# A linear-attention block and a gated MLP on one core: an x load cut in two, and the written-out instruction order searched again

## Chip, core and metric

The kernel runs on one core of one Trainium2 chip. The metric is device microseconds of one execution. The core has five engines that each work through their own instruction queue: TensorE (PE, matmuls, with its weight loads shown as PEld), VectorE (DVE), ScalarE (ACT), GpSimd (POOL) and SyncE (SP, which here only issues DMAs). They meet at semaphores alone.

## The reference

x is 2048 x 512 in bfloat16. Cut to what matters:

```python
x = A_x
h = x + A(layernorm(x))
out = h + B(layernorm(h))

def A(x):                       # 32 heads of 16
    q, k, v = split(x @ wqkv)
    pq, pk = phi(q), phi(k)     # phi(t) = where(t > 0, t + 1, exp(t)) + 1e-6
    kv, z = pk^T v, sum_s pk
    return ((pq kv) / (pq z + 1e-6)) @ wo

def B(x):                       # 1792 = 2 * 896
    z = gelu(x @ w_in)
    z1, z2 = z[:, :896], layernorm(z[:, 896:])
    return (z1 * (w_sp @ z2 + b_sp)) @ w_out
```

## The kernel before

The 2048 rows are 16 tiles of 128. Everything stays in SBUF. The stages, with the short names that the text uses and the line of the instruction:

- **Loads.** SP issues x tile 0, x tile 1, x tiles 2 and 3, the K weights `wk`, x 4 and 5, x 6 and 7, x 8 to 11, x 12 to 15, and the Q weights `wq`, in that order (`load_x`, `load`, L492). The other weights are loaded by POOL after the last x transpose has landed.
- **First layer norm.** For each tile, DVE takes `stats` (L567) and `aggr` (L571). The reciprocal root comes from ACT for tiles 0 to 3 (L581, L583) and from POOL for pairs of tiles from 4 on (`rstd_pool`: an add, L586, and a power, L588). DVE then makes `norm` (L603). Tiles 0 to 5 are transposed by PE (`T0` to `T5`, L633) and copied by ACT (`cp0` to `cp5`, L640). Tiles 6 to 15 are transposed by DMAs from SP (`T6` to `T15`, L625).
- **Attention.** `k0` to `k15` are the K projections of the tiles (L715, four matmuls each). They come in pairs, and `phi` of a pair goes through ACT (L692, L694) and DVE (L695, then L698 or L701). `kx` (L747, two matmuls each) accumulates k^T x of a tile and a half. `q0.0` to `q3.3` are the Q projections of a group of four tiles (L729), with their own `phi`. Then come the denominator (`den`, L829 and L844, with DVE L856 and L859 after it), the product with the values (L796), the output matrix (L814) and `o0` to `o15` (L879), whose residual is added on DVE (`resid`, L884).
- **Second layer norm.** `stats`, `aggr`, `rstd_pool`, and `minus` on POOL (L614, L615) give a bias, with which ACT makes `norm_h` (L610). SP transposes by DMA (`Th0` to `Th15`, L625).
- **MLP.** `z2` of a tile (L911) goes through GELU on ACT (L916), `stats` on DVE (L920), a reciprocal root on POOL and `norm` on DVE. `z1` (L942) is made by columns, with GELU at L947. `mix` (L981, 16 matmuls per 128 columns) multiplies with w_sp, DVE gates (L988), and `out` (L999) makes the result, to which DVE adds h (L1005).

PSUM has eight banks. A matmul group that needs a bank waits until the last reader of the bank's previous tile is done. POOL's reciprocal roots, ACT's copies and all else run in queue order: an instruction that waits holds up all behind it.

What each engine does next is written out, as a search made beforehand left it: `ORDER` is one list of all 803 operations, and each engine's queue is that list filtered by engine. `SLOT` gives each tile its place (a PSUM bank, an SBUF buffer). `schedule()` walks `ORDER` with the costs given to `op(...)` and a clock, but the clock only fills `start` and `end`. Queues, slots and waits follow from `ORDER`, `SLOT` and the data alone.

```python
for o in (self.ops[i] for i in ORDER):
    ...
    o.start, o.end = t, t + o.cost + o.lag
    ...
    order[o.eng].append(o)
```

Of the kernel before, what the change touches and what calls it, by code (L numbers as in the profile page):

```python
# [7 lines left out]
ACT = mybir.ActivationFunctionType  # L8
ALU = mybir.AluOpType
# [3 lines left out]


ORDER = [
# [36 lines left out]
]  # L52
SLOT = [
# [6 lines left out]
]  # L60


# [292 lines left out]
def bass_sequential_preLN__linear_attn_block__mixer_gmlp__prompt_kernel(  # L355
# [63 lines left out]
    pk = View(s_kv, 0, [NT, D], BF16)  # L419
# [18 lines left out]
    zb = small([KD * CG], BF16)  # L438
    sel = small([P], BF16)
    ones = small([CG], BF16)  # L440
    part = small([CG], BF16)
# [18 lines left out]
    zr_v = View(s_wsp, NT * GW * 2, [D], BF16)  # L460
# [18 lines left out]
    op = g.op  # L479
# [4 lines left out]
    def act_c(n, ptr=0):  # L484
        return 0.055 + 0.000833 * n + 0.093 * ptr
# [16 lines left out]
    def load_x(eng, a, b, bias=BIG, **kw):  # L502
        more = {2: 103e3, 4: 70e3}.get(a, 0)
        xl[a] = load(eng, f"x{a}", x[a:b, :], x_dram[a * P:b * P, :].rearrange("(n p) d -> p n d", p=P),
                     int((b - a) * P * D * 2 + more), bias, **kw)
# [4 lines left out]
    load("sp", "wk", wqkv[:, D:2 * D], w3[:, :, D:2 * D], D * D * 2 + 50000)  # L510
    for a in (4, 6):
        load_x("sp", a, a + 2)
    for a in (8, 12):
        load_x("sp", a, a + 4)
    load("sp", "wq", wqkv[:, 0:D], w3[:, :, 0:D], D * D * 2)
    for a, b in zip(g.ops, g.ops[1:]):
        b.after.append(a)
# [4 lines left out]
       r=[ident.all()], w=[ident.all()], bias=BIG)  # L522
# [62 lines left out]
    def rstd_pool(var, dst, n):  # L585
        op("pool", 0.25, lambda e: e.tensor_scalar(dst.ap(), var.ap(), EPS_LN, None, op0=ALU.add), r=[var], w=[dst])  # L586
        h = nhalf[0:n]
        return op("pool", 0.35, lambda e: e.tensor_tensor(dst.ap(), dst.ap(), h.ap(), ALU.pow), r=[dst, h], w=[dst],  # L588
                  lag=0.45)

    def stats_act(n):
        src, s1, nm, s2 = x[n, :], st_x[n, 0:1], st_x[n, 6:7], st_x[n, 7:8]
# [14 lines left out]


    def normalise_act(dst, src, rs, nm, n=512):
        op("act", act_c(n, 2), lambda e: e.activation(dst.ap(), src.ap(), ACT.Identity, bias=nm.ap(), scale=rs.ap()),  # L610
           r=[src, rs, nm], w=[dst])

    def minus(m, rs, nm):
# [33 lines left out]
    for grp in LN1:  # L647
        rs = small([len(grp)], FP32)
# [88 lines left out]
    for p in range(NP):  # L737
        t = kv_proj(p, D)
# [15 lines left out]
    tz = Tile(PS)  # L754

    def zsum(e):
# [2 lines left out]
            i = e.matmul(tz(bank(0)).ap()[CG * c:CG * (c + 1), :], lhsT=ones.ap, rhs=pk.ap[:, n, :],  # L759
                         start=(n < KD), stop=(n >= NT - KD), skip_group_check=True)  # L760
        return i
    op("pe", 1.02, zsum, r=[pk.all(), ones.all()], w=[tz()])
    for f in (0, 2):
        q_proj(0, f)

# [1 line left out]
       w=[zr_v.all()])  # L767
    tzT = Tile(PS)

    def zmm(e):  # L770
# [1 line left out]
            i = e.matmul(tzT(bank(0)).ap()[:, c * CG:(c + 1) * CG], lhsT=zr_v.ap[:, c * P:(c + 1) * P], rhs=part.ap,  # L772
                         start=(c == 0), stop=True, skip_group_check=True)
        return i
    op("pe", 0.25, zmm, r=[zr_v.all(), part.all()], w=[tzT()])

    def zmask(e):
        z = tzT(bank(0)).ap()[:, 0:KD * CG].rearrange("p (c f) -> p c f", c=KD)
# [4 lines left out]
    for h in range(2):  # L783
        d = xk_v[2 * h:2 * h + 2, :]
        if h == 0:
            op("act", act_c(1024), lambda e, h=h, d=d: e.activation(d.ap(), txk[h]().ap(), ACT.Copy), r=[txk[h]()],
               w=[d])
# [21 lines left out]
    for b in range(2):  # L809
        t = Tile(PS, 2)  # L810
        for i in range(2):
            c = 2 * b + i
            r_ = wo[c, :]
            op("pe", MM, lambda e, t=t, i=i, c=c, r_=r_: e.matmul(  # L814
                t(bank(i)).ap(), lhsT=kvT.ap()[:, c * P:(c + 1) * P], rhs=r_.ap(), start=True, stop=True),
               r=[kvT, r_], w=[t()])
# [6 lines left out]
    def den(gq):  # L823
        t = Tile(PS)
        r_ = pqT[gq].all()

        def mm(e):
            for c in range(KD):
                i = e.matmul(t(bank(0)).ap()[CG * c:CG * (c + 1), :], lhsT=zb.ap[:, CG * c:CG * (c + 1)],  # L829
                             rhs=r_.ap()[:, c, :], start=True, stop=True)  # L830
            return i
        op("pe", 0.33, mm, r=[zb.all(), r_], w=[t()])
        rr, rb = rr_v[gq, :], rb_v[gq, :]
        op("act", act_c(512, 1), lambda e: e.activation(rr.ap(), t(bank(0)).ap(), ACT.Ln, bias=eps[1:2].ap(),
                                                        scale=1.0), r=[t(), eps[1:2]], w=[rr])
        o = op("act", act_c(512), lambda e: e.activation(rb.ap(), rr.ap(), ACT.Exp, scale=-1.0), r=[rr],
               w=[rb])
        last_lnexp.append(o)
        spread = {0: Tile(PS, 2), 2: Tile(PS, 2)}

        def sp_(e):
# [2 lines left out]
                k = e.matmul(spread[c // 2 * 2](bank(c % 2)).ap(), lhsT=sel.ap[q0:q0 + CG, :],  # L844
                             rhs=rb.ap()[q0:q0 + CG, :], start=True, stop=True)
            return k
        op("pe", 0.33, sp_, r=[sel.all(), rb], w=[spread[0](), spread[2]()])
        for c0 in (0, 2):
            t2 = spread[c0]
            d = pqT[gq][c0:c0 + 2, :]  # L850
            if (gq, c0) in VIA_ACT:
# [3 lines left out]
                   r=[t2()], w=[b_])  # L855
# [13 lines left out]
    for gq in range(NG):  # L869
        g.bias = -GROUP * gq  # L870
        for p in (2 * gq, 2 * gq + 1):
            t = Tile(PS, 2)
# [205 lines left out]
```

## Time and profile before

| what | value |
|---|---|
| median of 3 runs | 245.82 us (244.99 to 247.24) |
| the profiled execution | 246.68 us |
| its span, first to last instruction | 244.9 us |
| granted TensorE clock | 1.00 |
| DVE, ACT, POOL busy | 135.5, 85.0, 32.8 us |
| matmuls, start to start in a full run of them | 0.216 us for 512 columns, 0.162 for 384 |

The profile is of one execution. Its page gives busy time by engine, its chain of waits follows the work back from the last instruction, the wait view says which engine stood idle for whom, and the timeline gives each instruction's start, duration, idle time before it in brackets and what ended that idle time. Windows give busy time per engine in a stretch. The view of DMA issues gives the time from issue to landing.

### The profile page before, as it was taken

The page shows a single profiled execution, that of the slowest core. Times are in us where ns is not written, and L with a number is a line of the kernel's source. Part 1 is how long each engine was busy: PE and PEld are TensorE (multiplying, and loading weights), DVE is VectorE, ACT ScalarE, POOL GpSimd, SP SyncE. Part 2 cuts the span into 40 slices and gives each one's busy share as a digit, 9 for nine tenths or more (in the row PEclk, how much of TensorE's full clock was granted, in tenths as well). Part 3 has the DMA queues.
Part 4 walks back from the last instruction along what each step waited for, and adds up shares of the span by engine and source line. Part 5 has one row for each costly group of instructions (what it writes and reads, how often), then busy time and mean ns, then how long its engine had stood idle before and what let it go on. Part 6 is the DMA issues. An engine that isn't in the chain of part 4 may idle for free.

```text
span 244.9 us, 3021 instructions
## 1 busy us (share of the span) xinstructions
PE 238.6 (97%) x1175; PEld 108.5 (44%) x1175; DVE 135.5 (55%) x269; ACT 85.0 (35%) x107; POOL 32.8 (13%) x87
## 2 busy tenths in 40 slices
PE   8798999999999998999999999999999999999995
PEld 3343443353444444444444444444444444444443
DVE  4899655679999694688523132252332523322443
ACT  3674756787599936855501100000000000000000
POOL 5114130000525305133200000000000000000000
DMA  6903368943123530479544454445000110000022
GB/s 199 313 4 74 80 122 332 252 106 67 35 55 64 120 72 3 88 210 146 90 95 103 94 84 104 107 98 137 3 0 0 46 43 0 0 0 3 0 86 86
DMA packets 55582, 21.57 MB, mean 88 GB/s; under 512 B 49456, under 2 KB 54704, under 8 KB 55568
## 3 DMA queue, kind: packets, MB, share of 16 engines
q1 hardware_dynamic: 54624, 17.05, 31.9%
q0 software_dynamic: 944, 4.33, 5.3%
q8 instruction: 9, 0.15, 0.3%
q14 instruction: 5, 0.04, 0.0%
HBM read 7.47 MB, written 2.10 MB: 39 GB/s over the span
## 4 chain that ended last, share of the span: by engine, by line
PE 73%; DVE 13%; ACT 5%; DMA 4%; POOL 2%; issue 1%; SPq 1%
PE ps L981 39%; PE ps L999 10%; PE ps L942 5%; PE ps L911 5%; DVE small L567 4%; PE ps L729 4%; PE ps L747 4%; DVE xh L884 3%; DMA xh<-in_A_x_dram 3%; PE ps L715 3%; ACT xn L610 2%; PE ps L879 2%; DMA xT_pq_z<-pk_xn_z 1%; DVE small L920 1%; POOL small L588 1%
## 5 line engine op out<-in xcount | busy, mean ns | idle before, releaser
L981 PE MATMUL ps<-wsp,pk_xn_z 128*128 128x512 bf16 x336 | 73.5, 379 | 0.0
L988 DVE TENSOR_TENSOR e<-ps,e 128x512 bf16<-128x512 f32 x28 | 19.4, 692 | 68.7 <-PE ps L981 68.7
L981 PEld LDWEIGHTS ps<-wsp,pk_xn_z 128*128 128x128 bf16 x336 | 32.9, 98 | 39.6
L942 PE MATMUL ps<-hT,win 128*128 128x512 bf16 x112 | 26.5, 379 | 0.7 <-ACT pk_xn_z L916 0.7
L911 PE MATMUL ps<-win,hT 128*128 128x512 bf16 (+1 forms) x128 | 26.2, 353 | 0.0
L999 PE MATMUL ps<-wout,xT_pq_z 128*128 128x512 bf16 (+1 forms) x119 | 24.7, 366 | 0.0
L981 PE MATMUL ps<-wqkv_wsp,pk_xn_z 128*128 128x512 bf16 x112 | 24.3, 379 | 0.0
L567 DVE BATCH_NORM_STATS2 small<-xh 128x6 f32<-128x512 bf16 x32 | 21.0, 681 | 4.0 <-DMA xh<-in_A_x_dram 3.8
L920 DVE BATCH_NORM_STATS2 small<-pk_xn_z 128x6 f32<-128x512 bf16 (+1 forms) x32 | 18.4, 611 | 7.7 <-ACT pk_xn_z L916 7.6
L692 ACT ACTIVATE e<-ps 128x1024 bf16<-128x1024 f32 x16 | 16.4, 1026 | 12.3 <-PE ps L715 6.5
L947 ACT ACTIVATE xT_pq_z<-ps 128x1024 bf16<-128x1024 f32 (+1 forms) x16 | 14.2, 911 | 18.5 <-PE ps L942 18.5
L911 PEld LDWEIGHTS ps<-win,hT 128*128 128x128 bf16 x128 | 12.5, 98 | 12.6 <-issue 0.2
L1005 DVE TENSOR_TENSOR e<-ps,xh 128x512 bf16<-128x512 f32 (+1 forms) x17 | 11.2, 660 | 11.3 <-PE ps L999 11.2
L999 PEld LDWEIGHTS ps<-wout,xT_pq_z 128*128 128x128 bf16 x119 | 11.7, 98 | 12.7
L916 ACT ACTIVATE pk_xn_z<-ps 128x896 bf16<-128x896 f32 x16 | 14.5, 916 | 7.7 <-PE ps L911 7.6
L981 PEld LDWEIGHTS ps<-wqkv_wsp,pk_xn_z 128*128 128x128 bf16 x112 | 11.0, 98 | 13.2
L942 PEld LDWEIGHTS ps<-hT,win 128*128 128x128 bf16 x112 | 10.7, 98 | 13.7 <-ACT pk_xn_z L916 1.7
L715 PE MATMUL ps<-wqkv_wsp,xT_pq_z 128*128 128x512 bf16 x64 | 15.8, 379 | 0.7 <-DMA xT_pq_z<-pk_xn_z 0.7
L588 POOL TENSOR_TENSOR small<-small 128x2 f32<-128x2 f32 x22 | 16.0, 732 | 1.3
L747 PE MATMUL ps<-pk_xn_z 128*128 128x512 bf16 x64 | 15.9, 379 | 0.0
L729 PE MATMUL ps<-xT_pq_z,wqkv_wsp 128*128 128x512 bf16 x64 | 15.6, 379 | 0.1
L879 PE MATMUL ps<-pk_xn_z,xT_pq_z 128*128 128x512 bf16 x64 | 14.8, 379 | 0.0
(72 smaller groups left out, 180.8 us busy)
## 6 DMA issues: line engine op xcount, KB each, us to landing
out_dram<-e SPq DMA_DIRECT2D x15, 128.0 KB, 1.7
win<-in_B_w_in_dram POOLq DMA_DIRECT2D x1, 1792.0 KB, 8.3
wqkv_wsp<-in_A_wqkv_dram SPq DMA_DIRECT2D x2, 512.0 KB, 6.3
xh<-in_A_x_dram SPq DMA_DIRECT2D x2, 512.0 KB, 7.1
wout<-in_B_w_out_dram POOLq DMA_DIRECT2D x1, 896.0 KB, 6.4
xh<-in_A_x_dram SPq DMA_DIRECT2D x3, 256.0 KB, 4.4
wsp<-in_B_w_sp_dram SPq DMA_TRANSPOSE x48, 3.0
wqkv_wsp<-in_A_wqkv_dram POOLq DMA_DIRECT2D x1, 512.0 KB, 8.8
```

What stands on the lines that cost most here:

```text
L567: op("dve", dve_c(512), lambda e: e.bn_stats(s6.ap(), src.ap()), r=[src], w=[s6])
L588: return op("pool", 0.35, lambda e: e.tensor_tensor(dst.ap(), dst.ap(), h.ap(), ALU.pow), r=[dst, h], w=[dst], lag=0.45)
L715: i = e.matmul(t(bank(ti)).ap(), lhsT=lhs.ap()[:, c, :], rhs=rhs.ap()[:, c, :], start=(c == 0), stop=(c == KD - 1))
L729: r_ = e.matmul(t(bank(i)).ap(), lhsT=lhs.ap()[:, c, :], rhs=rhs.ap()[:, c, :], start=(c == 0), stop=(c == KD - 1))
L747: r = e.matmul(txk[h](bank(i)).ap(), lhsT=xx.ap()[:, c * P:(c + 1) * P], rhs=kk.ap(), start=(n == 0), stop=(n == NT - 1))
L879: i = e.matmul(t(bank(ti)).ap(), lhsT=l.ap()[:, c, :], rhs=mw[c, :].ap(), start=(c == 0), stop=(c == KD - 1))
L911: k = e.matmul(t(bank(i)).ap()[:, 0:b - a], lhsT=l.ap()[:, c, :], rhs=win[c, a:b].ap(), start=(c == 0), stop=(c == KD - 1))
L920: op("dve", dve_c(b - a), lambda e, s6=s6, src=src: e.bn_stats(s6.ap(), src.ap()), r=[src], w=[s6])
L942: k = e.matmul(t(bank(i)).ap(), lhsT=l.ap()[:, c, :], rhs=r_.ap()[:, c, :], start=(c == 0), stop=(c == KD - 1))
L981: k = e.matmul(t(bank(0)).ap(), lhsT=l.ap()[:, s - a, :], rhs=r_.ap()[:, s - a, :], start=(s == 0), stop=(s == NT - 1))
L988: op("dve", dve_c(512), lambda e: e.tensor_tensor(gb().ap(), t(bank(0)).ap(), bsp().ap()[:, tg * GW:(tg + 1) * GW], ALU.add), r=[t(), bsp( ...
L999: k = e.matmul(t(bank(0)).ap()[:, 0:b - a], lhsT=l.ap()[:, fc, :], rhs=wout[fc, a:b].ap(), start=(fc == 0), stop=(fc == KF - 1))
```

## The change

One load becomes two. The rest of the SP queue is the same.

```diff
-    for a in (8, 12):
-        load_x("sp", a, a + 4)
+    for a in (8, 10):
+        load_x("sp", a, a + 2)
+    load_x("sp", 12, 16)
```

Costs that `schedule()`'s clock reads are edited: POOL's power from 0.35 with a lag of 0.45 to 0.7, `normalise_act` by +0.04, the small matmul groups L759, L772, L829 and L844 to 0.88, 0.1, 0.23 and 0.23 with other landing times.

```diff
-        return op("pool", 0.35, lambda e: e.tensor_tensor(dst.ap(), dst.ap(), h.ap(), ALU.pow), r=[dst, h], w=[dst],
-                  lag=0.45)
+        return op("pool", 0.7, lambda e: e.tensor_tensor(dst.ap(), dst.ap(), h.ap(), ALU.pow), r=[dst, h], w=[dst])
```

`ORDER` and `SLOT` are replaced as wholes. Because of the added load, operations from number 7 on are one higher. The same 803 other operations are there, each on its engine. Decoded into the names above, the queues differ most in these stretches (an arrow marks where a queue goes on):

```
PE  before: T0 warm warm T1 warm k0 warm T2 k1 T3 k2 T4 k3 T5 k4 kx0.1 kx1.1 q0.2 q0.3 k5 q0.0 kx2.1 kx3.1 q0.1
            kx0.0 kx1.0 kx2.0 kx3.0 kx4.0 k6 k7 kx4.1 kx5.1 kx5.0 q1.2 q1.3 k8 k9 ->
PE  after:  T0 warm warm T1 warm warm k0 T2 k1 k2 T3 T4 T5 k3 k4 q0.0 q0.1 k5 kx0.0 kx0.1 kx1.1 kx1.0 q0.2 q0.3
            kx2.0 kx3.0 kx2.1 kx3.1 k6 k7 kx4.1 kx5.1 q1.2 q1.3 kx4.0 kx5.0 q1.0 q1.1 kx6.0 k8 k9 ->
DVE before: stats6 stats11 norm4 norm5 phi_k0 aggr6 phi_k0 stats10 stats8 aggr11 stats7 stats13 aggr7 phi_k1
            stats14 phi_k1 norm6 aggr14 norm7 ->
DVE after:  stats6 stats7 norm4 norm5 aggr6 aggr7 phi_k0 stats15 phi_k0 norm7 stats12 aggr15 norm6 phi_k1 stats11
            aggr12 stats9 stats8 stats13 aggr8 aggr13 phi_k1 phi_k2 stats10 phi_k2 ->
POOL before (2nd layer norm, pairs): h0 h1, h3 and h2 mixed, h5, h4 and z0 mixed, bsp load, z2, h7 and h6 mixed, z4 ->
POOL after: h0 h1 h2, bsp load, h3 h6, add h4, minus h4, power h4, add z0, add z2, add h7, power z0, power h7,
            minus h7, minus h4, minus h7, power z2, h5, z4 ->
ACT after:  ... norm_h8 norm_h9 gelu1_1.6 gelu1_1.4 gelu2_7 norm_h14 gelu2_4 norm_h10 ->
PE  after, late: ... z2_6 z2_5 z1_1.6 z1_1.4 z1_1.5 z2_7 z2_4 z1_1.2 z1_1.3, first four matmuls of mix 0.0 ->
```

In the later part, the Q projections run in the order q0, q1, q3, q2 (before: q0 to q3), and the first `mix` group, which is cut into pairs of matmuls, starts among the `z2` of tiles 6 to 9 (before: after nearly all of `z2`). From `mix` 0.1 on both orders are the same but for four `z1` groups that stood behind `mix` 0.3, of which one remains, behind `mix` 0.5. POOL's constants at the start are in another order; the identity for the PE transposes is next to last but one.

More of the change, by code (lines that the diff above doesn't have):

```diff
@@ L609, in normalise_act @@
     def normalise_act(dst, src, rs, nm, n=512):
-        op("act", act_c(n, 2), lambda e: e.activation(dst.ap(), src.ap(), ACT.Identity, bias=nm.ap(), scale=rs.ap()),
+        op("act", act_c(n, 2) + 0.04, lambda e: e.activation(dst.ap(), src.ap(), ACT.Identity, bias=nm.ap(), scale=rs.ap()),
            r=[src, rs, nm], w=[dst])
@@ L761, in zsum @@
         return i
-    op("pe", 1.02, zsum, r=[pk.all(), ones.all()], w=[tz()])
+    op("pe", 0.88, zsum, r=[pk.all(), ones.all()], w=[tz()], land=3.0)
     for f in (0, 2):
@@ L774, in zmm @@
         return i
-    op("pe", 0.25, zmm, r=[zr_v.all(), part.all()], w=[tzT()])
+    op("pe", 0.1, zmm, r=[zr_v.all(), part.all()], w=[tzT()])
     def zmask(e):
@@ L831, in mm @@
             return i
-        op("pe", 0.33, mm, r=[zb.all(), r_], w=[t()])
+        op("pe", 0.23, mm, r=[zb.all(), r_], w=[t()], land=3.0)
         rr, rb = rr_v[gq, :], rb_v[gq, :]
@@ L846, in sp_ @@
             return k
-        op("pe", 0.33, sp_, r=[sel.all(), rb], w=[spread[0](), spread[2]()])
+        op("pe", 0.23, sp_, r=[sel.all(), rb], w=[spread[0](), spread[2]()], land=4.0)
         for c0 in (0, 2):
```

84 rows, old and new, of tables (ORDER, SLOT) are left out of this document.

## The prediction

> **What bounds the kernel now.** I read the page's busy times first, then PE's waits, then the timeline around each place where PE stands, then the views of DMA issues.
>
> ```profile
> PE 238.6 (97%) x1175; PEld 108.5 (44%) x1175; DVE 135.5 (55%) x269; ACT 85.0 (35%) x107; POOL 32.8 (13%) x87
> ```
>
> PE is the bound, and the change takes no matmul away. Only the time in which PE stands can be won.
>
> ```profile
> PE ps L633 <- DVE pk_xn_z L603: 1.4, 2, 1.1
> PE ps L555 <- PEq L1063: 0.8, 1, 0.8
> PE ps L942 <- ACT pk_xn_z L916: 0.7, 1, 0.7
> PE ps L715 <- DMA xT_pq_z<-pk_xn_z: 0.7, 1, 0.7
> ```
>
> The 0.8 is the start. The rest has three causes, shown by the timeline of the first 24 us and of 91 to 98.5:
>
> ```profile
> 10.34 0.69 DVE L567 BATCH_NORM_STATS2 small<-xh 128x6 f32<-128x512 bf16 x1 [0.81 <-DMA xh<-in_A_x_dram]
> 11.41 0.40 PE L633 MATMUL ps<-small,pk_xn_z 128*128 128x128 bf16 x4 [1.13 <-DVE pk_xn_z L603]
> 23.48 0.82 PE L715 MATMUL ps<-wqkv_wsp,xT_pq_z 128*128 128x512 bf16 x3 [0.66 <-DMA xT_pq_z<-pk_xn_z]
> 95.68 1.52 ACT L610 ACTIVATE xn<-xh,small 128x512 bf16<-128x512 bf16 x2 [1.52 <-POOL small L615]
> 98.05 0.82 PE L942 MATMUL ps<-hT,win 128*128 128x512 bf16 x3 [0.74 <-ACT pk_xn_z L916]
> ```
>
> First, stats11 waits for x 8 to 11 with norm4 queued behind it, and T4 waits for norm4. Second, k7 waits for T7. Third, ACT waits for POOL's bias and PE for the bank that ACT holds. Matmul ends are modelled, so I measure a stall by starts: gap between two starts, less the pitch (0.216 us for 512 columns).
>
> - T1 (6.63 after 6.07), with one warm-up moved ahead of k0: k0 starts 6.98 and could start 6.82, and one warm-up of 0.11 no longer follows it. 0.27.
> - T4: 11.41 - 9.91 - 0.22 = 1.29.
> - k7: 23.48 - 22.44 - 0.22 = 0.82.
> - q1.0 (37.98 after 37.52): 0.25.
> - 78.3 and 85.3: 0.18 each, 0.36.
> - z1 at 98.05 after 96.93: 1.12 - 0.22 = 0.91.
>
> Together 3.9 us. That is all there is to win, 1.6% of 245.8.
>
> **The change, part by part.**
>
> *Costs.* Only the clock of `schedule()` reads them, and it orders nothing: 0 exactly.
>
> *The load.* SP issues one DMA more, at a pitch of 0.52 us (x 8 at 3.74, x 12 at 4.26). The queue is full then: the first matmul that needs `wq` comes after 12.8, and the issues end at 5.8. What can move is landing. From issue times and issue views: x 4 lands at 7.10, x 6 at 7.81, x 8 to 11 at 10.32, x 12 at 11.82, `wq` at 13.14. A 256 KB load takes 0.71 behind another, so a pair takes 1.42. A 512 KB load took 2.51, 1.50 and 1.32. The split is thus worth between -1.09 (1.42 - 2.51) and +0.52 (one issue pitch, should the queue run dry). I take 0, because the loads are bound by bytes: the rows near it, 1.50 and 1.32, lie around 1.42.
>
> The Trainium skill, "DMA: Bandwidth & Descriptors", sections "Anatomy of one DMA" and "Rules for kernel authors", speaks against the split: about 2.0 us of fixed cost per DMA (its fit is for DMAs from GpSimd), so coalesce. If that were added behind a full queue, `wq` would land at 15.1 and the sum below would come to about 0. The 0.71 between x 4 and x 6 disagrees: 0.6 of it is 256 KB at its 436 GB/s.
>
> *The new order, to 21 us.* I walk the new queues with durations of this trace: stats 0.60 from start to start, norm 0.32, aggr 0.10, phi on DVE 0.33 with 0.59 (L698) or 1.14 (L701), ACT copies 0.59 and 1.02, k and q 0.86, kx 0.43, T 0.22; from the last matmul's group start to ACT 1.06 for k, 0.42 for T. A hop is 0.05.
>
> DVE comes to stats6 at 8.84 as before. Now stats7 follows (its tile landed at 7.81), so norm4 starts at 10.08 (POOL's power is done at 9.81), norm5 at 10.39. PE has k1, k2, T3 done by 9.85: T4 at 10.53, T5 at 10.86, stalls 0.68 and 0.11. Then k3 at 11.08 and k4 at 11.94 to 12.81. q0.0 now comes before k5 and needs `wq`: 13.19, a stall of 0.38. Before, k4 ended at 13.60 and q0.2 came at 14.46, after `wq`.
>
> On DVE, stats15 stands in front of the second part of phi_k0 and waits for x 12 to 15 (11.82). It ends at 12.45, the second part of phi_k0 at 13.59, norm7, stats12 and aggr15 follow, and norm6 starts at 14.62. So T6 is issued at 15.05 in place of 17.65. Its issue took 2.3 us and T7 landed 3.43 after its own: T7 lands at 20.8, where it was 23.43. PE reaches k6 at 20.98 and k7 at 21.84, so k7's stall is gone, with 1.0 to spare. The closest wait there is k6 for a bank of phi_k2, free at 20.76.
>
> *From 21 to 60.* T8 to T15 are issued at 23.3 to 32.2 (norm8 at 22.85, norm11 at 26.6), pitch 1.3, latency 2.46. The last lands at 34.7 (34.38 before), while k8 to k15 now run 28.3 to 38.3: at least 2.2 to spare. phi_k4 is just in time for kx8 (33.04 against 33.07). kx12 waits for phi_k6 0.23 (q1.0 did so before, 0.25). POOL's weight loads start at 34.9, as before: `wv` first, needed at 46.4 (landed 44.50, behind `win`), `wo` at 48.6 (46.26). L796 waits 0.12 for DVE's copy, and q2.2 waits 0.10 for a bank that ACT's second phi of q3 holds.
>
> *From 60 to 122.* Th0 and Th1 land at 64.3 and 65.6, and z2 of tile 1 comes at 67.0. GELU frees banks with 0.05 to 1.0 to spare, and z2_2 waits about 0.05. The load of b_sp moves from 82.0 to 74.0. It holds transposes up: Th8, issued 0.6 after it, took 4.36. Now that is Th4, landing at about 79.0, with z2 of tiles 6 and 5 due at 83.1. POOL: minus h4 is done at 86.15 and ACT takes norm_h8 at 86.6, so the 0.91 falls away. The PE matmuls of `mix` 0.0 put among z2 need norm z3 at 92.9 (done 89.0) and, last, norm z15 at 121.5 (120.0).
>
> *The late part.* All later matmuls are back to back before, and the same: 0. POOL's constants: all 18 were done by 4.5, T0 comes at 5.74: 0.
>
> *Sum.* Of 3.9 us, the new order pays back 0.68 + 0.11 + 0.38 early, 0.23 + 0.12 + 0.10 in the middle, and about 0.3 in waits of 0.05 and less: 1.9. Gain 2.0. As a check by position: `mix` 0.0 ends at 122.0 with one z1 group to come; before it ended at 121.4 with four; 121.4 + 3 x 0.864 = 124.0.
>
> The profiled execution took 246.68, so it would take 244.7. It lies 0.86 above the median of the runs, and I take the difference from the median: 245.82 - 2.0 = **243.8**.
>
> **The rivals.**
>
> *The early stalls go too.* The 0.68 and 0.11 hang on one DVE chain, the 0.38 on the last bytes of `wq`. DMA engines are 90% busy until 11.2 and nearly idle from 11.6, with `wq` landing only at 13.14: one straggler. Were it gone, and the chain 0.6 shorter, the gain would be 2.0 + 1.0: 242.8. For it: x 8 landing 1.0 later than its size explains. Against: nothing in the change touches a straggler.
>
> *The split and the order win nothing.* In the new order x 10 and x 11 are wanted at 15.25 and x 8 and 9 at 15.95, where one load of four lands at 10.32. So the split itself is hidden, and only stats11's new place removes the wait. If the excess of x 8's load (1.09) comes back at `wq`, q0.0 pays it in full and 0.9 is left (244.9); from `wq` at 15.2, two of it, the gain is spent: 245.8. For it: the excess is in the trace. Against: total bytes and their rate stay. The skill's rule above would end here too.
>
> *POOL's queue, slower than before.* minus h4 now stands behind an add that waits for aggr h15 (83.6 in my walk). norm_h8 on ACT waits for it, and behind norm_h8 the GELUs that free z2_4's and z1_1.2's banks. There is 0.45 on ACT and 1.0 on PE to spare. If aggr h15 is late by x, PE loses x - 1.45. Before, POOL stood for DVE in this way 4.8 us at most in 60 to 100 (L614 for L571), and PE paid 0.91. With 4.8: 3.35 lost, 247.2. It eats the gain from 3.45 on, and every us above is paid in full. DVE is the fullest engine beside PE there, 32.3 of 36 us in 60 to 96, which speaks for it. Against: aggr h15 then waits for no other engine in my walk, and it was 9 us later before (92.2).
>
> **How the numbers follow.** The forecast, 2.0 won with 0.8 more or less (243.0 to 244.6), has 0.42. The early stalls gone has 0.18, nothing won 0.18, POOL's queue 0.22. About 1% (2.46 us) is what a measurement of this kernel can tell from no change. Faster by more, under 243.36: the second case and two fifths of the forecast, 0.35. Slower by more, over 248.28, needs aggr h15 late by 5.9 or the waits behind it to add up: three fifths of that case, 0.13. The rest, 0.52, is within 1%. The range, 242.2 to 247.5, leaves out those 0.13 and some 0.04 below, where all 3.9 would be gone (241.9).
>
> **What would show it.** Right: no PE wait for norm4 longer than 0.7; stats11 without a DMA wait; q0.0 waiting for `wq` about 0.4; T6 issued near 15; k7 starting without a wait; ACT at norm_h8 not waiting for POOL; PE's last matmul near 240.4. Wrong: `wq` landing after 14; DVE standing over 0.5 at stats15 for x 12; PE waiting for GELU's banks between 68 and 118 in more than two places; a wait of ACT for L615 of over 1.5.

## The result and the profile after

The kernel after takes 244.22 us (median of 7 runs, 243.96 to 244.40), the kernel before 246.37 in 7 runs beside it (244.99 to 247.24). The ratio is 0.9921, with a 95% interval of 0.9897 to 0.9946: 2.15 us less. That is within the 1% which the prediction took for the least that a measurement can tell, but the interval excludes 1. In the later sets of 20 to 30 runs each the kernel before has medians of 245.86 to 246.02, so the gain is between 1.6 and 2.2. The spread of the runs fell with it: 2.25 us before, 0.44 after.

The profiled execution after took 243.96 us with a span of 242.2. The one before took 246.68 with a span of 244.9, so the two traces differ by 2.72, which is more than the medians do.

First the page's busy times of the kernel after (busy us, share of the span, instructions), then its list of PE's waits (total us, how often, longest), which has two rows:

```profile
PE 238.3 (98%) x1175; PEld 108.8 (45%) x1175; DVE 135.2 (56%) x269; ACT 85.1 (35%) x107; POOL 34.1 (14%) x87
```

```profile
PE ps L556 <- PEq L1063: 0.8, 1, 0.8
PE ps L633 <- DVE pk_xn_z L603: 0.4, 1, 0.4
```

PE's work is unchanged (238.6 before). The 0.8 is the start. Of the three causes named before, only T4's wait for norm4 is left, and it is down from 1.1 to 0.4; the rows of L942 (the bank that ACT held) and of L715 (k7 waiting for T7) are gone. By starts less pitch, as in the prediction, the stalls left after are k0 0.19, T4 0.54, T5 0.09, q2.2 0.10 and the group of L844 0.19: 1.1 us, where before shows 3.97. The difference, 2.9, accounts for the 2.72 within the 0.2 that such sums can't resolve.

Each of the three places in the timeline of the kernel after (start, duration, engine, line, operation; idle time before in brackets; some line numbers are one higher than before):

```profile
8.94 1.28 DVE L568 BATCH_NORM_STATS2 small<-xh 128x6 f32<-128x512 bf16 x2
10.13 0.72 DVE L603 TENSOR_SCALAR pk_xn_z<-xh,small 128x512 bf16<-128x512 bf16 x2
10.59 0.72 PE L633 MATMUL ps<-small,pk_xn_z 128*128 128x128 bf16 x8 [0.38 <-DVE pk_xn_z L603]
11.23 0.69 DVE L568 BATCH_NORM_STATS2 small<-xh 128x6 f32<-128x512 bf16 x1
12.87 1.89 PE L729 MATMUL ps<-xT_pq_z,wqkv_wsp 128*128 128x512 bf16 x8
...
20.64 1.89 PE L715 MATMUL ps<-wqkv_wsp,xT_pq_z 128*128 128x512 bf16 x8
...
84.53 0.49 POOL L615 TENSOR_TENSOR small<-small 128x2 f32<-128x2 f32 x2
85.78 1.51 ACT L610 ACTIVATE xn<-xh,small 128x512 bf16<-128x512 bf16 x2
```

What counts here is the brackets that are missing. stats6 and stats7 run as one pair (x2 at 8.94) and norm4 and norm5 follow at 10.13, not at 10.96. stats15 (11.23) doesn't wait for its load. q0.0 (12.87) doesn't wait for `wq`, which landed at 12.35. k6 and k7 (20.64) run as eight matmuls in one row. POOL's minus h4, the first of the two at 84.53, ends at 84.72, and ACT takes norm_h8 at 85.78 without standing for it.

What this gave back by stretch is in the view of windows (stretch, its length, busy us of PE, PEld, DVE, ACT, POOL with instruction counts, clock, DMA share, GB/s). The kernel before:

```profile
0.00:24.00 24.00, 21.10 (x105) 9.42 (x106) 19.96 (x53) 13.80 (x23) 8.30 (x32) 1.00 0.51 149
96.00:122.00 26.00, 25.26 (x126) 12.07 (x124) 17.13 (x40) 17.15 (x21) 6.89 (x13) 1.00 0.63 122
```

The kernel after:

```profile
0.00:24.00 24.00, 22.77 (x112) 10.33 (x113) 20.69 (x54) 15.43 (x25) 10.37 (x34) 1.00 0.49 145
96.00:122.00 26.00, 26.00 (x129) 12.50 (x128) 15.70 (x37) 14.97 (x18) 5.79 (x11) 1.00 0.62 127
```

PE is busy 1.67 us more in the first 24 us and 0.74 more between 96 and 122, where it now has no gap at all. That is 2.4 of the 2.7.

### The profile page after: what moved, and what is told of

Same layout as the page of the kernel before. It is cut to its first block, busy times and chain, and to the rows that moved or that the text cites. A ratio compares the mean times of both kernels' runs of the same rounds, so it can differ in the third digit from the quotient of the medians.

```text
span 242.2 us, 3026 instructions
## 1 busy us (share of the span) xinstructions
PE 238.3 (98%) x1175; PEld 108.8 (45%) x1175; DVE 135.2 (56%) x269; ACT 85.1 (35%) x107; POOL 34.1 (14%) x87
## 4 chain that ended last, share of the span: by engine, by line
PE 91%; DVE 4%; DMA 2%; ACT 2%; SPq 1%; issue 0%
PE ps L981 40%; PE ps L942 10%; PE ps L911 10%; PE ps L999 10%; PE ps L747 6%; PE ps L879 5%; PE ps L715 5%; PE ps L729 4%; DMA xh<-in_A_x_dram 2%; DVE small L568 1%; SPq L492 1%; DVE xT_pq_z L698 1%; DVE xh L884 0%; DVE xT_pq_z L859 0%; DVE e L695 0%; PE ps L844 0%
## 5 line engine op out<-in xcount | busy, mean ns | idle before, releaser
L942 PE MATMUL ps<-hT,win 128*128 128x512 bf16 x112 | 26.6, 379 | 0.0
L947 ACT ACTIVATE xT_pq_z<-ps 128x1024 bf16<-128x1024 f32 (+1 forms) x16 | 14.4, 913 | 23.9 <-PE ps L942 23.9
L942 PEld LDWEIGHTS ps<-hT,win 128*128 128x128 bf16 x112 | 10.9, 98 | 12.6 <-ACT pk_xn_z L916 0.4
L587 POOL TENSOR_SCALAR small<-small 128x2 f32<-128x2 f32 x22 | 6.4, 297 | 67.6 <-DVE small L572 67.4
L715 PE MATMUL ps<-wqkv_wsp,xT_pq_z 128*128 128x512 bf16 x64 | 15.3, 379 | 0.0
```

What stands on the lines that cost most here:

```text
L715: i = e.matmul(t(bank(ti)).ap(), lhsT=lhs.ap()[:, c, :], rhs=rhs.ap()[:, c, :], start=(c == 0), stop=(c == KD - 1))
L942: k = e.matmul(t(bank(i)).ap(), lhsT=l.ap()[:, c, :], rhs=r_.ap()[:, c, :], start=(c == 0), stop=(c == KD - 1))
```

## The experiments

Two theories stood after the result. Mine: the order of the queues wins all of it, by taking away T4's, k7's and z1's waits, and the split of the load wins nothing. The rival: the earlier landings in the trace after (x 8 at 8.69, where x 8 to 11 landed at 10.32 before; `wq` at 12.35, where it was 13.14) come from the split and are part of the gain. Medians below are of runs beside runs of the kernel before on the same chip.

**The split alone** (e1): the kernel before with the new loads and its old order.

```diff
-    for a in (8, 12):
-        load_x("sp", a, a + 4)
+    for a in (8, 10):
+        load_x("sp", a, a + 2)
+    load_x("sp", 12, 16)
```

> The kernel before with the load cut in two and its old order otherwise. Theory 'order' (the 2.15 us come from the queue order, the cut is worth only what it takes off one wait): stats11 then waits for x 10 and 11 alone, which landed at 9.45 in the changed kernel where stats6 ends at 9.5, so T4's stall of 1.29 falls to about 0.5; the stalls at k7 (0.82) and at the bank of GELU (0.91) stay: 0.8 won, about 245.6. If x 10 lands no earlier than x 8 to 11 did, nothing is won: 246.4. Rival 'landing' (loads land earlier by 0.8 because of the cut, and that is the gain): 2 us won, 244.3, with wq landing near 12.4.

Measured 245.73, ratio 1.0005 (0.9985 to 1.0026): nothing. x 8 and 9 landed at 9.33 and x 10 and 11 at 10.10, `wq` at 12.89. PE's waits of this kernel:

```profile
PE ps L634 <- DVE pk_xn_z L604: 0.8, 3, 0.3
PE ps L716 <- DMA xT_pq_z<-pk_xn_z: 0.8, 1, 0.8
PE ps L943 <- ACT pk_xn_z L917: 0.5, 1, 0.5
```

All three causes are there (lines one higher); only the longest wait for norm4 fell, from 1.1 to 0.3, and the median didn't follow.

**The order alone** (e2): the kernel after with x 8 to 11 in one load, as the kernel before has it.

```diff
-    for a in (8, 10):
-        load_x("sp", a, a + 2)
-    load_x("sp", 12, 16)
+    for a in (8, 12):
+        load_x("sp", a, a + 4)
```

> The changed kernel with x tiles 8 to 11 in one load again. Theory 'order': stats11 and stats9 come at 14.6 and 15.3, long after any landing, so the cut is hidden; only wq matters, and if it lands at 13.1 as before, q0.0 at 12.87 waits 0.3: 244.2 to 244.5. Rival 'landing': most of the gain goes, 246. In between would mean that x 12 to 15 and wq land later by more than 0.5.

Measured 244.01, ratio 0.9929 (0.9903 to 0.9954): all of the gain. The load of four landed as late as before, at 10.24, and `wq` at 13.07; q0.0 lost 0.11 to `wq`. T4 lost 0.70 (0.54 in the trace after), but not to that load: as in the kernel after, norm4 stands behind stats6 and stats7 alone. The rival falls.

**Single loads** (e5): the kernel after, with x 8 to 11 as four loads of 128 KB.

```diff
-    for a in (8, 10):
-        load_x("sp", a, a + 2)
+    for a in (8, 9, 10, 11):
+        load_x("sp", a, a + 1)
     load_x("sp", 12, 16)
```

> The changed kernel with x tiles 8 to 11 in four loads of one tile: two more DMAs in front of x 12 to 15 and wq. Theory 'bytes' (a load behind a full queue costs its bytes alone): wq lands between 12.3 and 13.1 as in all traces so far, 244.2. Rival 'fixed cost' (the Trainium skill, 'DMA: Bandwidth & Descriptors', section 'Anatomy of one DMA': about 2.0 us per DMA): wq lands about 4 us later, q0.0 waits 3.5, 247.7. A half of it would show as wq near 14.4 and 245.7.

Measured 243.92 (4 runs), ratio 0.9904 (0.9876 to 0.9932): not to be told from the kernel after. The view of DMA issues gives KB each and us from issue to landing. The kernel after:

```profile
xh<-in_A_x_dram SPq DMA_DIRECT2D x1, 512.0 KB, 6.2
wqkv_wsp<-in_A_wqkv_dram SPq DMA_DIRECT2D x1, 512.0 KB, 7.1
```

With single loads:

```profile
xh<-in_A_x_dram SPq DMA_DIRECT2D x4, 128.0 KB, 4.3
xh<-in_A_x_dram SPq DMA_DIRECT2D x1, 512.0 KB, 5.2
wqkv_wsp<-in_A_wqkv_dram SPq DMA_DIRECT2D x1, 512.0 KB, 6.1
```

Two DMAs more, issued 0.5 apart, put `wq`'s issue about 1.0 later and leave 1.0 less between issue and landing: it lands at 12.28 (12.35 after). The four land 0.37 apart, where 256 KB took 0.75 and 512 KB 1.50. In this queue, behind other loads, a load cost its bytes and no more that these traces show. The Trainium skill ("DMA: Bandwidth & Descriptors", "Anatomy of one DMA") gives about 2.0 us of fixed cost per DMA, fitted on DMAs from GpSimd. Were that paid by one load after the other, four loads would end 6 us later than one (an estimate, 3 x 2.0 of that page); here it doesn't add up in this way.

**One wait at a time** (e3, e4, e9). Each edits only DVE's, POOL's or ACT's queue of the kernel before. e3 takes stats11 out of norm4's way:

```diff
 DVE
-norm3 stats6 stats11 norm4 norm5 phi_k0 aggr6 phi_k0 stats10 stats8 aggr11 stats7  stats13 aggr7
+norm3 stats6 stats7  norm4 norm5 phi_k0 aggr6 phi_k0 stats10 stats8 aggr7  stats11 stats13 aggr11
```

> The kernel before, in which stats11 and stats7 (and their aggr) change places on DVE, and nothing else. Theory 'order': norm4 comes 0.83 earlier, T4's stall falls from 1.29 to about 0.5, norm6 and T6 come about 0.8 earlier too, as does PE, so k7 waits as before: 0.8 won, 245.6. Rival 'landing': DVE meets the late x loads at the next place (stats10, stats8), and nothing is won: 246.4.

Measured 245.82, ratio 0.9994 (0.9971 to 1.0017): nothing. The timeline of this kernel has these two waits:

```profile
10.65 0.40 PE L633 MATMUL ps<-small,pk_xn_z 128*128 128x128 bf16 x4 [0.25 <-DVE pk_xn_z L603]
...
22.82 1.04 PE L715 MATMUL ps<-wqkv_wsp,xT_pq_z 128*128 128x512 bf16 x4 [0.76 <-DMA xT_pq_z<-pk_xn_z]
```

T4's stall is down to 0.41, and k7's stays, at 0.92 (0.82 before). Trace against trace this is what the theory said: T6 is issued at 16.89 (17.65 before), k7 starts at 22.82 (23.48), and the span is 244.0 (244.9). The medians don't follow. What may explain it is a chance in the trace before: x 8 to 11 landed 2.51 after x 6 and 7 there. In the six other traces that have this single load (e2, e3, e4, e7, e9, e11) it landed 1.49 to 1.51 after them. In e1 and e4, which keep stats11 in its old place, DVE runs it right behind stats6, without a wait; there x 4 and 5 came late instead (7.86 and 8.09), and DVE stood 0.9 at stats4. So e3 takes away a wait that some executions don't have. That the median run of the kernel before doesn't have it either is argued from these traces, not shown.

e4 puts the bias of tiles 12 and 13 first, so that ACT needn't stand for POOL ahead of the z1 at 98.05:

```diff
 DVE
-stats_h12 stats_h13 ... aggr_h15 aggr_h14 normz2 aggr_h13 aggr_h12
+stats_h12 stats_h13 aggr_h12 aggr_h13 ... aggr_h15 aggr_h14 normz2
 POOL
-bsp load, power z2 twice, h7 and h6 mixed, z4
+bsp load, h6, power z2 twice, h7, z4
 ACT
-gelu2_9 norm_h14 norm_h12 gelu2_5
+gelu2_9 norm_h12 norm_h14 gelu2_5
```

> The kernel before, in which the bias of tiles 12 and 13 is made before that of 14 and 15: aggr h12 and h13 right after their stats on DVE, their four POOL instructions ahead of the root of z2, and norm_h12 ahead of norm_h14 on ACT. Theory 'order': ACT's wait of 1.52 for POOL goes, gelu2_5 ends at about 96.6 in place of 98.0, and the PE stall of 0.91 at 97 goes with it: 0.9 won, 245.5. Rival 'POOL's queue' (the wait comes back where POOL is needed next): 0 to 0.3 won.

Measured 245.39, ratio 0.9986 (0.9964 to 1.0007). PE's waits of this kernel have no row of L942 any more:

```profile
PE ps L633 <- DVE pk_xn_z L603: 0.8, 3, 0.3
PE ps L715 <- DMA xT_pq_z<-pk_xn_z: 0.6, 1, 0.6
```

The stall is gone from the trace, and no later wait takes its place; the time is 0.6 less by the medians, but the interval includes no change.

e9 also moves norm6 and norm7, and with them T6 and T7, ahead:

```diff
 DVE
-stats6 stats11 norm4 norm5 phi_k0 aggr6 phi_k0 stats10 stats8 aggr11 stats7 stats13 aggr7 phi_k1 stats14 phi_k1 norm6 aggr14 norm7
+stats6 stats7 norm4 norm5 phi_k0 aggr6 aggr7 phi_k0 stats10 stats8 norm6 norm7 stats11 stats13 aggr11 phi_k1 stats14 phi_k1 aggr14
```

> The kernel before with stats7 in stats11's place, aggr7 behind aggr6, and norm6 and norm7 behind stats8 on DVE; nothing else. In every trace so far where T6 and T7 were slow (T7 landing 5.5 to 5.9 us after T6's issue) one 16 KB fetch of instructions by DMA ran between 17.6 and 20.1, between T6's issue and T7's landing; in the two where they took 3.9 (the changed kernel, and it without the cut) both were over before the fetch at 19.2 to 19.7. Theory 'fetch': T6 issued near 15 takes 3.9 to T7's landing, k7's stall of 0.8 to 0.9 goes: 245.0, 0.9 won. Rival 'latency' (the first transposes are slow wherever they stand; what counts is only that T6 comes early): T7 lands at 20.6, k7's stall goes as well, and the time is the same, but the trace shows the 5.8. Rival 'absorbed': the stall comes back at the next phi: 245.9.

Measured 245.27, ratio 0.9987 (0.9965 to 1.0009). T6 was issued at 14.43 (17.65 before) and k7 doesn't wait. PE's waits:

```profile
PE ps L942 <- ACT pk_xn_z L916: 0.5, 1, 0.5
...
PE ps L911 <- DVE small L571: 0.3, 1, 0.3
```

Of the time saved early, z2 of the first tiles takes some back (a new stall of 0.44 at 70.23, for DVE). z1 still waits, 0.65 at 96.61, as it does in e1 and e3.

**All three at once** (e11): the edits of e9 and e4 together; PE's queue stays that of the kernel before.

> The kernel before with the edits of e9 and of e4 together, on DVE, POOL and ACT; PE's queue, the loads and all places stay as before. Theory 'three waits' (the whole gain of the changed kernel is these three waits, each one local): stalls of 0.8 at k7 and of 0.65 to 0.9 at the GELU bank go, and T4 no longer hangs on the x 8 to 11 load: 244.3, like the changed kernel. Rival 'the PE order' (the gain needs PE's new order): 245.3 or more.

Measured 244.53, ratio 0.9947 (0.993 to 0.9964): 1.3 us. Alone the two give 0.14% and 0.13%, neither of which can be told from nothing; together 0.53%, which can. By the medians they give 0.6 and 0.6, and 1.3 together. Whether the two are worth more together than one by one isn't told by these intervals. This is three to four fifths of the change, without a matmul moved. The rest, 0.3 to 0.9 us, must come with PE's own new order or the remaining moves of the new queues; I didn't test these apart.

The profiled execution of e11 is the slowest of its twelve (245.82), and its list of PE's waits starts with this row:

```profile
PE ps L633 <- DVE pk_xn_z L603: 2.1, 3, 1.5
```

k7's and z1's waits are gone, as meant. But x 4 and 5 landed only at 8.90 in this execution (7.10 in the trace before). norm3 stands behind stats4 and stats5, and T3 lost 1.68. So this DVE order frees T4 of the load of x 8 to 11, but not the early transposes of late loads.

**T6 late** (e10): the kernel after with norm7 and norm6 behind the second part of phi_k1.

```diff
 DVE
-stats15 phi_k0 norm7 stats12 aggr15 norm6 phi_k1 stats11 aggr12 stats9 stats8 stats13 aggr8 aggr13 phi_k1
+stats15 phi_k0 stats12 aggr15 phi_k1 stats11 aggr12 stats9 stats8 stats13 aggr8 aggr13 phi_k1 norm7 norm6
```

> The changed kernel with norm7 and norm6 moved on DVE from before the first part of phi_k1 to behind its last part; nothing else. T6 is issued at about 18 in place of 14.4, into the fetch of instructions at 19.2. Theory 'fetch': T6 lands at 21.3 and T7 at 23.7, k6 and k7 wait together about 2.2: 246.4. Rival 'no collision' (3.9 from T6's issue to T7's landing as in the changed kernel): T7 lands at 21.9, k7 waits 0.2 to 0.4: 244.5.

Measured 245.12, ratio 0.9973 (0.9959 to 0.9987), 0.9 over the kernel after. T6 is issued at 18.73 and T7 lands at 22.62. PE's waits:

```profile
PE ps L715 <- DVE small L572: 0.4, 1, 0.4
PE ps L715 <- DMA xT_pq_z<-pk_xn_z: 0.3, 1, 0.3
```

The first row is k6, which waits for two things that come within 0.03: T6, which landed at 21.23, and DVE; the view names the later one. The second is k7. k6 loses 0.52 and k7 0.43, which is the 0.9: it is DVE's place for norm6 and norm7 that took k7's wait away.

**POOL's power twice** (e6 after, e7 before): each root on POOL computes its power a second time, into a spare tile, which adds 0.7 us to POOL's queue for each. This is the test of the third rival.

```diff
-        return op("pool", ..., lambda e: e.tensor_tensor(dst.ap(), dst.ap(), h.ap(), ALU.pow), r=[dst, h], w=[dst])
+        twin = small([n], FP32)
+        return op("pool", ..., lambda e: [e.tensor_tensor(x_.ap(), dst.ap(), h.ap(), ALU.pow)
+                                          for x_ in (twin.all(), dst)][-1], r=[dst, h], w=[dst])
```

> The changed kernel with every power on POOL done twice (the first into an unused place): 22 more POOL instructions of 0.71. Theory 'slack': norm4 waits for the second power, T4 0.5 later; norm_h8's bias comes three powers later, 86.9 against 85.8 when ACT is free for it, of which PE has 1.0 to spare: 0.5 to 1.0 lost against the changed kernel, 244.7 to 245.2. Rival 'POOL's queue': PE waits at z2_4 and z1_1.2 for the full 2.1 and at later pairs again: 247 or more.

> The kernel before with every power on POOL done twice. Theory 'slack': the bias of tiles 12 to 15 stands behind two powers, so the GELU bank's stall of 0.7 to 0.9 grows by 1.4; norm_h4 on ACT, which stood 1.5 for POOL near 73, comes 1.4 later; T4 loses 0.4 where x 8 lands early: 1.5 to 2.2 lost, 247.4 to 248.1, more than the changed kernel loses. Rival 'same': it loses what the changed kernel loses, and the new order is no safer against a long power.

After: 246.12, ratio 1.0007 (0.9984 to 1.003), 1.9 lost, twice what I had expected at most. Before: 252.16 (4 runs), ratio 1.0229 (1.019 to 1.0267), 6.1 lost, nearly three times what I had expected at most. PE's waits with the longer power, the kernel after first (lines one higher) and then the kernel before:

```profile
PE ps L634 <- DVE pk_xn_z L604: 0.7, 1, 0.7
PE ps L943 <- ACT pk_xn_z L917: 0.4, 1, 0.4
PE ps L748 <- DVE pk_xn_z L699: 0.4, 1, 0.4
PE ps L912 <- ACT xT_pq_z L948: 0.3, 1, 0.3
```

```profile
PE ps L943 <- ACT pk_xn_z L917: 2.3, 1, 2.3
PE ps L748 <- DVE pk_xn_z L702: 1.3, 2, 1.0
PE ps L634 <- DVE pk_xn_z L604: 1.0, 2, 0.7
```

The row of L912 is the rival's place: z2_4 waits for the bank that gelu1 frees late (a stall of 0.48 at 90.67). So the mechanism is real, but it costs 0.48 under a power of twice the length and nothing under the real one. Under the same load the old order loses 2.46 at z1 alone. Not all of its 6.1 is waiting. Three of its four runs, the profiled one among them, have a granted clock of 0.993, the fourth has 1.000 and took 250.42. The page of the profiled one shows where the clock fell (tenths in 40 slices of the span):

```profile
PEclk9999999999999999799999999999999999999999
```

Soon after the stall at z1, from 103.4 to 106.4, matmuls of 512 columns start 0.427 us apart, in place of 0.216. That is worth about 1.5 us (an estimate from these starts: half of 3.0). In the one run with the full clock the old order loses 4.4, the new one 1.9 in its median. The new order bears a late POOL more than twice as well.

**Trying to beat it** (e8, e12). e8 gives the root of tiles 4 and 5 to ACT, so that norm4 needn't wait for POOL, and puts norm4 and norm5 ahead of stats7:

```diff
-    R_POOL = (4, 6, 8, 10, 12, 14)
+    R_POOL = (6, 8, 10, 12, 14)
 DVE
-norm3 stats6 stats7 norm4 norm5 aggr6
+norm3 stats6 norm4 norm5 stats7 aggr6
```

> The changed kernel with the reciprocal root of tiles 4 and 5 on ACT in place of POOL and norm4 and norm5 ahead of stats7 on DVE. T4's stall of 0.54 and T5's of 0.09 hang on POOL's power, done at 9.90, and on stats7. Theory 'chain': norm4 starts at about 9.55, T4 follows T3 at 10.05 without a wait: 0.5 to 0.6 won against the changed kernel, 243.6. Rival 'next wait': k3's copy on ACT comes 0.15 later behind the root and q0.0 then meets wq, which landed between 12.35 and 13.1: 0.1 to 0.3 won, 244.0.

Measured 243.94, ratio 0.9926 (0.9904 to 0.9949): not to be told from the kernel after. T4's stall fell from 0.54 to 0.22, and this is what took its place:

```profile
PE ps L715 <- ACT xT_pq_z L640: 0.3, 1, 0.3
```

k3 waits for the copy of T3, which stands behind phi_k0 on ACT (a stall of 0.42). e12 therefore moves the copies cp3 to cp5 ahead of phi_k0 on ACT, and stats15 ahead of it on DVE:

```diff
 ACT
-cp2 phi_k0 cp3 cp4 cp5 phi_k1
+cp2 cp3 cp4 cp5 phi_k0 phi_k1
 DVE
-stats7 aggr6 aggr7 phi_k0 stats15 phi_k0
+stats7 aggr6 aggr7 stats15 phi_k0 phi_k0
```

> The kernel of the last call with the root of tiles 4 and 5 on ACT, and the copies cp3 to cp5 ahead of phi_k0 on ACT, stats15 ahead of it on DVE. There T4 no longer waited, but k3 waited 0.42 for cp3, which stood behind phi_k0. Theory 'next wait': this 0.42 goes, phi_k0 ends 1.2 later with kx0 having 2 to spare: 243.5 to 243.7. Rival: T6 comes 0.6 later and meets the fetch of instructions, or wq is met: 244.0.

Measured 244.9, ratio 0.9953 (0.9935 to 0.9971): worse than both, where I had expected 243.5 to 244.0. k3's stall is gone, but now kx2.0 loses 0.57 to phi_k1 and k6 0.33 to a bank of phi_k2, and L814 1.19 to the load of `wo`. That trace is of the slowest of the nine runs (245.73), so not all of this need be in the median. With the copies first, phi_k0 on ACT starts at 11.52 (9.16 in the kernel after), and phi_k1 follows it. No kernel here is clearly faster than the one after.

## Why the prediction was right

The forecast was 243.8, measured 244.22; 2.0 won, measured 2.15 (1.6 to 1.8 against the larger sets). Most steps went the way that was forecast; several sizes were off, and they made up for one another.

- *The load at nothing*: right. e1 and e2 put it at zero from both sides, and of its bounds (-1.09 and +0.52) neither end came. The "excess" of 1.09 at x 8 to 11 wasn't the load's form: the same single load landed at 9.47, 9.67, 10.15, 10.24, 10.32, 10.33 and 11.12 in seven traces, and only in the trace before was it late against the load ahead of it. It is chance, as the straggler of the first rival had it.
- *T4 0.68 and T5 0.11 are left*: 0.54 and 0.09. The chain from POOL's power over norm4 was read rightly.
- *q0.0 waits 0.38 for `wq`*: not in the trace after, since `wq` landed 0.8 earlier by the same chance; 0.11 in e2, where it landed at 13.07.
- *T1 and k0, 0.27 won*: not won. T1's wait went, but k0 started at 7.00 (6.98 before). The warm-ups took 5.25 us in place of 4.92, and T0 came at 5.91 (5.74). k0 follows T0 through ACT's copy: without these 0.17 it would have come at 6.83, where the walk had 6.82. In e8, which has the same start of PE's queue, T0 came at 5.74 and k0 at 6.81.
- *T6 issued at 15.05, T7 landing at 20.8*: 14.38 and 18.26. The step's direction was right, k7's stall is gone, but the 3.43 from issue to landing, taken from the row before, was mis-sized: both took 2.5. The spare ahead of k7 is 3.2 us, not 1.0. So e10 could issue T6 4.35 later and lose only 0.9.
- *78.3 and 85.3, 0.18 each*: gone, but they were smaller. The first is a group of L844, which starts about 0.31 after the matmul ahead of it where nothing waits, so both were 0.13.
- *kx12 0.23, L796 0.12, q2.2 0.10*: the first two aren't there, the third is 0.10. The group of L844 lost 0.19, which I hadn't named.
- *The z1 bank, 0.91 gone*: right, and for the reason given. minus h4 was done at 84.7 (86.15 in the walk), norm_h8 began at 85.78 (86.6), and e4, which makes only that part of the move, takes the same stall away.
- *Late part the same*: right. `mix` 0.0 ended at 121.27 (122.0 in the walk), and the lead is 2.72 at PE's last matmul too (239.45, before 242.17).
- *The sum*: 1.9 was to remain, 1.1 did. That alone would make the gain too small by 0.8. Against it, the 1.29 at T4 was one execution's: e1 and e4, with the old place of stats11 too, show T3 and T4 together at 0.83 and 0.80. So I subtracted from the median a loss of about 0.5 that a median run, to judge by these two traces, doesn't have. The two errors nearly cancel, which is luck and not skill.

Of the rivals, *the early stalls go too* came true at `wq` and not at T4. *The split and the order win nothing* is refuted for the order by e2 and holds for the split. *POOL's queue* is real as a mechanism and absent with the power as it is (e6).

What the prediction missed is that its one trace held a late load, so that the largest stall of its list was partly that execution's own. e3, which removes T4's excess alone, wins 0.1 by the medians. e4 and e9, which remove z1's and k7's stalls, win 0.6 each, within their intervals of nothing, and together 1.3, which is clear.

## What to carry to other kernels

Before a stall is counted as gain, ask what the bound engine meets next and whether that too comes earlier. An edit that is worth a few tenths can stay within the noise while two of them together stand out, as e4, e9 and e11 do here. One profiled execution mixes chance into its waits; a wait on a load whose landing differs from its neighbours' pitch should be looked up in a second trace before its whole length enters a sum. An order can be tested for what it can bear by making one off-path operation longer in both kernels: the same 0.7 us per root cost 6.1 in the one (4.4 in the run that kept its full clock) and 1.9 in the other.

## What the runs showed of the hardware that was not expected

*DMA transposes that stand alone took 2.5 us, or from 3.0 to 4.4.* Away from the loads of weights, T6 and T7 took 2.5 us from issue to landing in some traces and 3.0 to 4.4 in others. The traces with the long ones have a 16 KB packet, of the queue that fetches instructions, between T6's issue and T7's landing. The DMA view of the kernel before from 17.66 to 22 us (packets, MB, share of the 16 engines; then the issue with its median):

```profile
q1 hardware_dynamic: 1077, 0.26, 34.7%
q8 instruction: 1, 0.02, 1.7%
...
xT_pq_z<-pk_xn_z SPq DMA_TRANSPOSE x3, 3.4
```

The kernel after from 14.4 to 18.2 us, with no such packet in it:

```profile
q1 hardware_dynamic: 1088, 0.26, 34.2%
...
xT_pq_z<-pk_xn_z SPq DMA_TRANSPOSE x2, 2.5
```

In the kernel before, T6 took 3.40 (17.65 to 21.05) with the packet from 18.33 to 19.52, and T7, held up behind it, 3.43. e1, e3 and e4 show the same; in e8 T7 took 4.16 with a packet at 17.93, and in e7 T6 2.98 with one at 18.73. In the kernel after, e2, e5, e6, e9, e11 and e12 no packet falls there, and both took 2.5. e10 was meant to force it and didn't: its packet came at 22.39, in the last 0.23 of T7, and both took 2.5 there too. So the two go together, and that the packet is the cause is argued, not shown. It bears on k7: from T6's issue to T7's landing the kernel after takes 3.88, and with this T7 would have landed at 21.53 in the trace before (an estimate, 17.65 + 3.88), ahead of k7's turn at 22.66. So the stall of 0.82 goes with the long T6 and T7; an earlier T6 leaves room for them. What sets its time (one every 15 to 32 us) stays open.

*The granted clock reads 1.00 while the first matmuls run at half pace.* The warm-ups start 0.427 us apart, against 0.216 later. That lasted to 5.05 in the trace before and to 5.91 in the trace after; in e3 it ended at 3.35. The Trainium skill, "TensorE: Matmul & The Clock Gate", "Wait — 56ns, not 53.3ns?", gives this pitch (426.7 ns at 512 columns) for a cold array, and the trace agrees. When it ends differs between traces with the same start of PE's queue (5.91 after, 4.63 in e8), so the 0.17 us at T0 isn't the change's. Later in the span the same view does show a fall, as in e7.
